# Mixer block with an MLP: the last output tile in three column pieces, and the instructions outside a block

## The chip, the cores and the metric

The kernel runs on one core of a Trainium2 chip. Its time is device time in microseconds (us), the median over several executions. The profile comes from one execution; its span runs from the first to the last recorded instruction of the program on that core. Engines are named as the profile names them: PE (matrix unit; PEld is its weight load), DVE (vector), ACT (activation), POOL (GpSimd) and SP (the engine that issues most DMAs).

## The reference

The input `x` has 2048 rows of 512 columns (bfloat16). Two stages follow one another:

```python
h  = gelu(layernorm(x) @ w1)                       # 512 -> 512
hs = concat(g0, g1, g2, g3) @ w2                   # four column quarters of h, shifted along the rows by +1, -1, +2, -2
x1 = x + hs
h2 = gelu(layernorm(x1) @ w3) @ w4                 # 512 -> 1792 -> 512
return x1 + h2
```

## The kernel before

The rows are cut into 16 tiles of 128. Stage 1 normalizes a tile (`ln`), transposes it, multiplies by `w1` (`mm_up`, layer 1) and evicts through the activation function into `hT`; `mm_mix` reads `hT` with shifted columns, multiplies by `w2`, and DVE adds `x`, which gives the tile `x1`. Stage 2 normalizes `x1`, multiplies by `w3` (`mm_up`, layer 2) into `h2T`, and `mm_down` multiplies by `w4`.

`mm_down(t)` is where an output tile is made. It is 14 matmuls on PE (one for each 128 rows of `w4`, line 511) that sum into one bank of `o_ps`, one DVE addition of `x1` that moves the sum to `o_sb` (line 519), and one store that SP issues (line 522). The last tile, 15, is made in column pieces whose widths stand in `TAIL`: each piece has its own bank, its own 14 matmuls `down15_0`, `down15_1`, its own addition `res15_0`, `res15_1` and its own store. The banks of `o_ps` are handed out in turn by `next_bank`, and there are two of them (`NOB = 2`).

The operations are not issued where they are written. `pg.add` records each with what it reads and writes, and `Program.order` puts them in an order for each engine: PE in the order of `SCRIPT`, which ends with `down:14-15`, the others by due times. `emit` then issues them in that order and places the waits. A wait is placed only where the engine does not already know that the event has come.

`emit` does this inside `nc.Block()`. The block gives each engine a body of its own; the engine's main body ends in a jump to it (lines 602 to 606), and the body ends in another jump (line 593) to a common end, where all five engines meet: each engine drains and reports to POOL on one semaphore, POOL waits for the four reports and then releases the four on another. A meeting of the same form also stands ahead of the kernel's first instruction (line 669); it belongs to the program's frame and not to `emit`. The last instructions of SP's body wait for the semaphore of every store (line 655).

Of the kernel before, what the change touches and what calls it, by code (L numbers as in the profile page):

```python
# [12 lines left out]
ENGINES = ["sp", "act", "pe", "dve", "pool"]  # L13
# [178 lines left out]
SQRT = (0,)  # L192
STAT_ACT = (1, 3, 6, 16, 23)
HALF = (0,)
TAIL = (256, 256)
LOADS = """
x2 x1 x0 x4-5 w1b w1a x3 w2 x6-7 w3 x8-11 x12-15 w4b tp19 w4a
"""
# [6 lines left out]
def bass_standalone__mixer_s_mlp__prompt_kernel(nc, x, w1, w2, w3, w4, out):  # L205
# [14 lines left out]
    with ExitStack() as es:  # L220
# [38 lines left out]
        def next_bank():  # L259
            nbank[0] += 1  # L260
            return (nbank[0] - 1) % NOB, nbank[0]
# [236 lines left out]
        def mm_down(t):  # L498
# [3 lines left out]
            c0 = 0  # L502
            for hh, W in enumerate(TAIL if last else (D,)):
                b, v = next_bank()
# [72 lines left out]
        pg.line(queue)  # L577
        pg.order()
        emit(nc, es, pg)

def emit(nc, es, prog):

    engs = {"sp": nc.sync, "act": nc.scalar, "pe": nc.tensor, "dve": nc.vector, "pool": nc.gpsimd}
    sems = {e: es.enter_context(nc.semaphore("sem_" + e)) for e in ENGINES}
    ndma = 0
    for op in prog.seq:
        if op.queue is not None:
            op.stream = ("dma", ndma)
            sems[op.stream] = es.enter_context(nc.semaphore(f"sem_dma{ndma}"))
            ndma += 1  # L590
        else:
            op.stream = op.eng
    with nc.Block() as block:
        bodies = {}

        def keep(name):
            def _body(e):
                bodies[name] = nc.cur_body

            return _body  # L600

        block.gpsimd(keep("pool"))
        block.sync(keep("sp"))
        block.scalar(keep("act"))
        block.vector(keep("dve"))
        block.tensor(keep("pe"))
        know = {e: {} for e in ENGINES}
        implied = {}
        count = {}
        last_write, readers = {}, {}  # L610
        for op in prog.seq:
            e = op.eng
            needs = {}

            def need(sv):
                if needs.get(sv[0], 0) < sv[1]:
                    needs[sv[0]] = sv[1]

            for res, ver in op.reads:
                lw = last_write[res]  # L620
                assert lw[2] == ver, (op.name, res, ver, lw)
                need(lw)
            for res, ver in op.writes:
                if res in last_write:
                    need(last_write[res])
                for sv in readers.get(res, ()):
                    need(sv)
            if e == "pe":
                needs.pop("pe", None)
            k = know[e]  # L630
            with nc.body(bodies[e]):
                for s, v in sorted(needs.items(), key=lambda sv: -sv[1]):
                    if k.get(s, 0) >= v:
                        continue
                    engs[e].wait_ge(sems[s], v)
                    for s2, v2 in implied[(s, v)].items():
                        if v2 > k.get(s2, 0):
                            k[s2] = v2
                    k[s] = max(k.get(s, 0), v)
                ins = op.fn(engs[e])  # L640
                inc = 1 if op.queue is None else 16
                ins.then_inc(sems[op.stream], inc)
            val = count[op.stream] = count.get(op.stream, 0) + inc
            snap = dict(k)
            snap[op.stream] = max(snap.get(op.stream, 0), val)
            implied[(op.stream, val)] = snap
            for res, ver in op.reads:
                readers.setdefault(res, []).append((op.stream, val))
            for res, ver in op.writes:
                last_write[res] = (op.stream, val, ver)  # L650
                readers[res] = []
        with nc.body(bodies["sp"]):
            for op in prog.seq:
                if op.name.startswith("out_dma"):
                    nc.sync.wait_ge(sems[op.stream], 16)


# [26 lines left out]
```

## Time and profile before

| what | us |
|---|---|
| median of 9 runs | 138.47 |
| lowest and highest of them | 137.95 and 139.11 |
| span of the profiled execution | 137.3 |
| the profiled execution's own time | 139.1 |

| engine | busy us | share of the span |
|---|---|---|
| PE | 131.4 | 96% |
| DVE | 58.8 | 43% |
| ACT | 51.4 | 37% |
| POOL | 19.5 | 14% |

The granted clock of PE is 0.999 of full speed. The time of an execution is 1.8 us longer than its span: what is done before the program's first recorded instruction and after its last lies outside the span. Waits and the issue of DMAs are not counted as busy; they are read from the views of single lines and of the waits. Records of sequencers carry a q (SPq, POOLq, PEldq).

### The profile page before, as it was taken

How to read it: one execution, taken by the hardware profiler on the slowest of the kernel's cores; microseconds unless marked ns; L12 is line 12 of the kernel's file. 1: busy time of each engine (PE TensorE's matmuls, PEld its weight loads, DVE VectorE, ACT ScalarE, POOL GpSimd, SP SyncE). 2: the span in 40 equal slices, each digit the busy share in tenths (PEclk: the TensorE clock that was granted, in tenths of full speed). 3: DMA queues.
4: the chain of work that ended last, by engine and by line, in shares of the span. 5: the costliest groups of instructions: out<-in, count | busy, mean ns of one | idle time of the engine just before them, and what ended most of it. 6: DMA issues, size and time to landing. Idle time of an engine off the chain costs nothing.

```text
span 137.3 us, 1989 instructions
## 1 busy us (share of the span) xinstructions
PE 131.4 (96%) x786; PEld 72.9 (53%) x786; DVE 58.8 (43%) x169; ACT 51.4 (37%) x70; POOL 19.5 (14%) x43
## 2 busy tenths in 40 slices
PE   6689999989999999999999999999999999999992
PEld 2287788756668644444444444444444444444471
DVE  1888899996899650044520053220002222322231
ACT  4799657432757545540055520025550000000000
POOL 2341483331142510001010000000000000000000
PEclk9999999999999999999999999999999999999999
DMA  3999964583279542001210002110001111111111
GB/s 111 299 357 410 354 212 98 115 81 76 40 183 205 114 99 54 0 0 38 81 38 1 0 0 70 44 38 5 0 0 36 40 38 38 43 38 38 67 48 41
DMA packets 21257, 12.19 MB, mean 89 GB/s; under 512 B 13568, under 2 KB 20736, under 8 KB 21248
## 3 DMA queue, kind: packets, MB, share of 16 engines
q1 hardware_dynamic: 21104, 12.00, 33.8%
q8 instruction: 6, 0.10, 0.3%
q10 hardware_dynamic: 144, 0.07, 0.2%
q14 instruction: 3, 0.02, 0.1%
HBM read 6.82 MB, written 2.10 MB: 65 GB/s over the span
## 4 chain that ended last, share of the span: by engine, by line
PE 83%; DVE 6%; DMA 5%; POOL 2%; SPq 1%; issue 1%; ACT 0%
PE y_ps L442 39%; PE o_ps L511 35%; PE o_ps L482 8%; DMA xnT<-xn_buf 3%; DVE st L349 3%; DMA x_sb<-in_x_dram 2%; POOL rstd L366 2%; DVE xn_buf L372 1%; PE y_ps L415 1%; POOL xn_buf L383 1%; SPq L296 1%; DVE mv L351 0%; DVE vpe L355 0%; DVE st6b L343 0%; DVE xnT L421 0%
## 5 line engine op out<-in xcount | busy, mean ns | idle before, releaser
L442 PE MATMUL y_ps<-xnT,w_sb 128*128 128x256 bf16 (+2 forms) x440 | 64.3, 305 | 0.5 <-DMA xnT<-xn_buf 0.5
L442 PEld LDWEIGHTS y_ps<-xnT,w_sb 128*128 128x128 bf16 x440 | 40.2, 98 | 24.6 <-issue 1.2
L511 PE MATMUL o_ps<-w_sb,h2T 128*128 128x512 bf16 (+1 forms) x238 | 48.9, 366 | 0.0
L457 ACT ACTIVATE h2T<-y_ps 128x1024 bf16<-128x1024 f32 (+1 forms) x29 | 28.6, 994 | 36.6 <-PE y_ps L442 36.6
L511 PEld LDWEIGHTS o_ps<-w_sb,h2T 128*128 128x128 bf16 x238 | 23.3, 98 | 25.3
L519 DVE TENSOR_TENSOR o_sb<-o_ps,x_sb 128x512 bf16<-128x512 f32 (+1 forms) x17 | 11.2, 660 | 44.6 <-PE o_ps L511 44.3
L366 POOL TENSOR_TENSOR rstd<-vpe,neghalf 128x1 f32<-128x1 f32 x31 | 17.0, 559 | 62.3 <-DVE vpe L355 50.3
L493 DVE TENSOR_TENSOR x_sb<-o_ps,x_sb 128x512 bf16<-128x512 f32 x14 | 9.6, 689 | 22.9 <-PE o_ps L482 22.9
L349 DVE BATCH_NORM_STATS2 st<-x_sb 128x6 f32<-128x512 bf16 x26 | 17.5, 685 | 2.2 <-DMA x_sb<-in_x_dram 2.1
L482 PE MATMUL o_ps<-w_sb,hT 128*128 128x512 bf16 x64 | 15.9, 379 | 0.0
L372 DVE TENSOR_SCALAR xn_buf<-x_sb,mv,rstd 128x512 bf16<-128x512 bf16 x25 | 10.2, 412 | 3.9 <-POOL rstd L366 2.8
L457 ACT ACTIVATE hT<-y_ps 128x1024 bf16<-128x1024 f32 (+1 forms) x10 | 8.4, 851 | 8.3 <-PE y_ps L442 8.2
L482 PEld LDWEIGHTS o_ps<-w_sb,hT 128*128 128x128 bf16 x64 | 6.1, 98 | 5.3
L535 PE MATMUL o_ps<-zeros 128*128 128x512 bf16 x12 | 4.1, 514 | 1.2 <-DVE zeros L269 1.2
L380 ACT ACTIVATE xn_buf<-x_sb,nmr,rstd 128x512 bf16<-128x512 bf16 x5 | 4.0, 810 | 2.6 <-DVE nmr L376 2.6
L351 DVE BATCH_NORM_AGGREGATE mv<-st 128x2 f32<-128x6 f32 x26 | 4.1, 173 | 0.2
L355 DVE TENSOR_SCALAR vpe<-mv 128x1 f32<-128x1 f32 x26 | 3.6, 148 | 0.3
L415 PE MATMUL y_ps<-ident,xn_buf 128*128 128x128 bf16 x28 | 2.4, 220 | 1.3 <-DVE xn_buf L372 1.2
L324 ACT ACTIVATE junk<-x_sb 128x512 bf16<-128x512 bf16 x5 | 3.1, 629 | 0.7 <-DVE x_sb L489 0.7
L535 PEld LDWEIGHTS o_ps<-zeros 128*128 128x128 bf16 x12 | 1.4, 125 | 3.4 <-issue 1.9
L415 PEld LDWEIGHTS y_ps<-ident,xn_buf 128*128 128x128 bf16 x28 | 1.8, 98 | 2.4 <-DVE xn_buf L372 2.0
L420 ACT ACTIVATE xnT<-y_ps 128x512 bf16<-128x512 bf16 (+1 forms) x5 | 2.6, 549 | 0.1
(33 smaller groups left out, 18.9 us busy)
## 6 DMA issues: line engine op xcount, KB each, us to landing
out_dram<-o_sb SPq DMA_DIRECT2D x15, 128.0 KB, 1.7
w_sb<-in_w_dram SPq DMA_DIRECT2D x1, 1792.0 KB, 9.8
w_sb<-in_w_dram SPq DMA_DIRECT2D x2, 896.0 KB, 9.4
x_sb<-in_x_dram SPq DMA_DIRECT2D x2, 512.0 KB, 11.3
x_sb<-in_x_dram SPq DMA_DIRECT2D x2, 256.0 KB, 4.5
w_sb<-in_w_dram SPq DMA_DIRECT2D x2, 256.0 KB, 3.5
w_sb<-in_w_dram SPq DMA_DIRECT2D x1, 512.0 KB, 5.6
x_sb<-in_x_dram SPq DMA_DIRECT2D x3, 128.0 KB, 2.4
```

Of the source, the lines that this page charges most:

```text
L349: pg.add("dve", f"bnst{q}", lambda e: e.bn_stats(st6[:, q, :], src), reads=rs, writes=[(("st6", q), 0)], dur=605)
L351: pg.add("dve", f"bnag{q}", lambda e: e.bn_aggr(mv[:, q, :], st6[:, q, :]), reads=[(("st6", q), 0)], writes=[(("mv", q), 0)], dur=75)
L366: lambda e: e.tensor_tensor(col(rstd), col(vpe), neghalf[:], ALU.pow),
L372: lambda e: e.tensor_scalar(dst, src, mv[:, q, 0:1], rstd[:, q : q + 1], ALU.subtract, ALU.mult),
L415: ins = e.transpose(chunk(c), xn_buf[:, slot(q), P * c : P * (c + 1)], ident[:])
L442: ins = e.matmul(y_ps[:, p, W * i : W * (i + 1)], wsb[:, dc, P * fc : P * (fc + 1)], src[:, dc, P * t0 : P * t0 + W], start=(dc == 0), sto ...
L457: (lambda d, s: (lambda e: e.activation(d, s, ACT_F.Gelu_apprx_tanh)))(dst, ysrc),
L482: ins = e.matmul(dst, hT[:, j, c0 : c0 + P], w2_sb[:, j, :], start=(j == 0), stop=(j == DC - 1))
L493: f = lambda e: e.tensor_tensor(x1_sb[:, t, :], dst, x_sb[:, t, :], ALU.add)
L511: ins = e.matmul(dst, h2T[:, fc, P * t : P * (t + 1)], w4_sb[:, fc, cs], start=(fc == 0), stop=(fc == FC - 1))
L519: (lambda d, c: (lambda e: e.tensor_tensor(o_sb[:, oi, c], d, x1_sb[:, t, c], ALU.add)))(dst, cs),
L535: ins = e.matmul(o_ps[:, b, :], zeros[:, 0:P], zeros[:], start=True, stop=True)
```

## The change

`TAIL` becomes `(256, 128, 128)`: the first piece of the last tile stays as it is, and the second is made as two pieces of 128 columns, each with 14 matmuls, an addition and a store. The third piece gets the bank that the first one had.

`emit` no longer opens a block. The same loop issues into the main body of each engine, so the five jumps at lines 602 to 606, the five at line 593 and the meeting of the engines at the end are gone. SP's waits for the stores are its last instructions; there are 18 stores instead of 17. The program's order on each engine is otherwise the same.

```diff
-TAIL = (256, 256)
+TAIL = (256, 128, 128)
...
-    with nc.Block() as block:
-        bodies = {}
-
-        def keep(name):
-            def _body(e):
-                bodies[name] = nc.cur_body
-
-            return _body
-
-        block.gpsimd(keep("pool"))
-        block.sync(keep("sp"))
-        block.scalar(keep("act"))
-        block.vector(keep("dve"))
-        block.tensor(keep("pe"))
-        know = {e: {} for e in ENGINES}
...
-            with nc.body(bodies[e]):
-                for s, v in sorted(needs.items(), key=lambda sv: -sv[1]):
...
-                    engs[e].wait_ge(sems[s], v)
...
-                ins = op.fn(engs[e])
...
-        with nc.body(bodies["sp"]):
-            for op in prog.seq:
-                if op.name.startswith("out_dma"):
-                    nc.sync.wait_ge(sems[op.stream], 16)
+    know = {e: {} for e in ENGINES}
...
+        for s, v in sorted(needs.items(), key=lambda sv: -sv[1]):
...
+            engs[e].wait_ge(sems[s], v)
...
+        ins = op.fn(engs[e])
...
+    for op in prog.seq:
+        if op.name.startswith("out_dma"):
+            nc.sync.wait_ge(sems[op.stream], 16)
```

More of the change, by code (lines that the diff above doesn't have):

```diff
@@ L592, in emit @@
             op.stream = op.eng
-    with nc.Block() as block:
-        bodies = {}
-        def keep(name):
-            def _body(e):
-                bodies[name] = nc.cur_body
-            return _body
-        block.gpsimd(keep("pool"))
-        block.sync(keep("sp"))
-        block.scalar(keep("act"))
-        block.vector(keep("dve"))
-        block.tensor(keep("pe"))
-        know = {e: {} for e in ENGINES}
-        implied = {}
-        count = {}
-        last_write, readers = {}, {}
-        for op in prog.seq:
[L612 to L630, printed above, removed]
-            with nc.body(bodies[e]):
-                for s, v in sorted(needs.items(), key=lambda sv: -sv[1]):
-                    if k.get(s, 0) >= v:
-                        continue
-                    engs[e].wait_ge(sems[s], v)
[L636 to L639, printed above, removed]
-                ins = op.fn(engs[e])
[L641 to L651, printed above, removed]
-        with nc.body(bodies["sp"]):
-            for op in prog.seq:
-                if op.name.startswith("out_dma"):
-                    nc.sync.wait_ge(sems[op.stream], 16)
@@ new lines, in emit, with need @@
+    know = {e: {} for e in ENGINES}
+    implied = {}
+    count = {}
+    last_write, readers = {}, {}
+    for op in prog.seq:
+        e = op.eng
+        needs = {}
+        def need(sv):
+            if needs.get(sv[0], 0) < sv[1]:
+                needs[sv[0]] = sv[1]
+        for res, ver in op.reads:
+            lw = last_write[res]
+            assert lw[2] == ver, (op.name, res, ver, lw)
+            need(lw)
+        for res, ver in op.writes:
+            if res in last_write:
+                need(last_write[res])
+            for sv in readers.get(res, ()):
+                need(sv)
+        if e == "pe":
+            needs.pop("pe", None)
+        k = know[e]
+        for s, v in sorted(needs.items(), key=lambda sv: -sv[1]):
+            if k.get(s, 0) >= v:
+                continue
+            engs[e].wait_ge(sems[s], v)
+            for s2, v2 in implied[(s, v)].items():
+                if v2 > k.get(s2, 0):
+                    k[s2] = v2
+            k[s] = max(k.get(s, 0), v)
+        ins = op.fn(engs[e])
+        inc = 1 if op.queue is None else 16
+        ins.then_inc(sems[op.stream], inc)
+        val = count[op.stream] = count.get(op.stream, 0) + inc
+        snap = dict(k)
+        snap[op.stream] = max(snap.get(op.stream, 0), val)
+        implied[(op.stream, val)] = snap
+        for res, ver in op.reads:
+            readers.setdefault(res, []).append((op.stream, val))
+        for res, ver in op.writes:
+            last_write[res] = (op.stream, val, ver)
+            readers[res] = []
@@ L659 @@
+    for op in prog.seq:
+        if op.name.startswith("out_dma"):
+            nc.sync.wait_ge(sems[op.stream], 16)
 _INS = ['x', 'w1', 'w2', 'w3', 'w4']
```

## The prediction

> **What bounds the kernel now.** I read the page's first part, then the chain of waits, the timeline of the last microseconds, and last the single lines of the end (655 and 593), which hold no busy time and so show in no sum.
>
> From the page, the span and the engines' busy time:
>
> ```profile
> span 137.3 us, 1989 instructions
> PE 131.4 (96%) x786; PEld 72.9 (53%) x786; DVE 58.8 (43%) x169; ACT 51.4 (37%) x70; POOL 19.5 (14%) x43
> ```
>
> PE fills the span except at its two ends, and the change touches only the ends. The chain in order of time (start, length, what):
>
> ```profile
> 0.72 0.39 SPq L296
> ...
> 1.64 2.96 DMA x_sb<-in_x_dram
> 4.62 0.43 DVE st6b L343
> ...
> 101.34 33.29 PE o_ps L511 x168
> 134.65 0.42 DVE o_sb L519
> ```
>
> It begins with SP's issue of the first loads, so what delays that issue delays everything. It ends with 33.29 us of unbroken PE and the last addition. What follows is not in the chain: 137.3 - (134.65 + 0.42) = 2.2 us of store and parting. The timeline of the last tile (start, length, engine, line, operation, then the idle time before it):
>
> ```profile
> 131.65 0.69 DVE L519 TENSOR_TENSOR o_sb<-o_ps,x_sb 128x512 bf16<-128x512 f32 x1 [2.39 <-PE o_ps L511]
> 133.12 0.42 DVE L519 TENSOR_TENSOR o_sb<-o_ps,x_sb 128x256 bf16<-128x256 f32 x1 [0.78 <-PE o_ps L511]
> 134.65 0.42 DVE L519 TENSOR_TENSOR o_sb<-o_ps,x_sb 128x256 bf16<-128x256 f32 x1 [1.10 <-PE o_ps L511]
> ```
>
> The two pieces are 1.53 us apart, PE's time for 14 matmuls of 256 columns. SP issues the last store at 135.10. Lines 655 (SP's waits for the stores) and 593 (the block's end), by instruction, with first and last start:
>
> ```profile
> L655 SPq EVENT_SEMAPHORE  x8: 28/28/28, 135.5 to 136.9; - x8
> L593 POOLq EVENT_SEMAPHORE  x2: 17/17/17, 137.1 to 137.2; - x2
> L593 SPq COMPARE_BRANCH  x1: 33/33/33, 136.9 to 136.9; - x1
> L593 SPq DRAIN  x1: 7/7/7, 137.1 to 137.1; - x1
> L593 PEldq EVENT_SEMAPHORE  x1: 51/51/51, 137.2 to 137.2; - x1
> ```
>
> SP's wait for the last store ends at 136.88 in the trace (last semaphore event at 136.84). Then come the jump at 136.92, SP's drain at 137.08, POOL's gathering at 137.11 and its release at 137.19, the last release at 137.24 plus 0.05. All of it, 137.30 - 136.88 = 0.41 us, stands after the last useful event.
>
> [...] The trace has 692 ns for 512 columns and 424 for 256[...]. [...] The jumps leave no record of their own here, but SP's release from the first meeting starts at 0.64 and lasts 0.02, and its first load is issued at 0.72: 0.07 us, room for one. [...]
>
> **The change, part by part** (against the profiled execution: span 137.30, time 139.1).
>
> *Five jumps at the start.* SP issues its first load one jump earlier[...] between 0 and the 0.07 that the trace has between release and issue. The chain above starts with this issue, so the shift is passed on whole; DVE, PE, ACT and POOL move with it.
>
> *PE in the tail.* Fourteen matmuls of 256 columns become 28 of 128. The pace at 128 columns is in the trace, from an early stage:
>
> ```profile
> 7.90 1.28 PE L442 MATMUL y_ps<-xnT,w_sb 128*128 128x128 bf16 x20
> ```
>
> A single one takes 0.22, so the pace is (1.28 - 0.22)/19 = 0.056 us, and 28 x 0.056 = 1.56 against 14 x 0.109 = 1.53 before: +0.04. Weight loads double to 28 at 98 ns each, and overlap as in that row.
>
> *The new bank wait.* `down15_2` takes the bank of `down15_0` and so waits for `res15_0`, which ends at 133.12 + 0.42 = 133.55. PE comes there at 132.92 (start of the second piece) + 14 x 0.056 = 133.70. From a DVE end to a waiting PE the trace has 0.05 (the memset of `zeros` ends at 1.11, PE starts at 1.16), so 0.10 us of cover is left and the wait costs nothing. Without it, `down15_2` with its 14 matmuls, then `res15_2` and the last store, would be late by as much. `res15_1` (from about 133.9 for 0.29) is done before `res15_2` is due at about 134.69.
>
> *DVE in the tail.* The last addition is 128 wide[...].
>
> *The last store.* SP issues three stores instead of two, 0.33 us each and over 0.7 us apart, so none queues behind another. The issues' sizes and median times to landing:
>
> ```profile
> out_dram<-o_sb SPq DMA_DIRECT2D x15, 128.0 KB, 1.7
> out_dram<-o_sb SPq DMA_DIRECT2D x2, 64.0 KB, 1.6
> ```
>
> By single issue the trace has 1.69 for most of 128 KB, 1.53 for the first of 64 KB, and 1.73 for the last, whose last semaphore event comes 0.17 after the one before it while a refill of instructions (8 KB, from 136.27 to 136.68) is under way. From 1.69 to 1.53 the 64 KB are worth 0.16, so 32 KB save 0.08. Packets of 256 B to HBM are not in the trace: bounds -0.25 (the late event goes too) and +0.25 (each packet costs twice its 27 ns at 512 B, 8 to an engine: 8 x 27 = 0.22). I take -0.08.
>
> *The end.* SP's nine waits of two semaphores each (one more than before) run about 0.06 us apart during the 1.6 us in which the last store is on its way; only the last counts, and with it the program ends. Jump, drains, gathering and release go: -0.41. The bounds are 0[...] and -0.9: the 0.41 and half a microsecond of what PE, DVE, ACT and POOL do after the program, which they now reach before SP does. I take -0.41 with the 1.8 us outside the span unchanged.
>
> Sum: -0.05 + 0.04 - 0.13 - 0.08 - 0.41 = **-0.63 us**, a span of 136.67. The profiled execution's 139.1 stands 0.6 above the median of the runs; the difference is carried over to the median: 138.47 - 0.63 = **137.84 us**, -0.45%.
>
> **The rivals.**
> 1. *The end costs the same elsewhere.* [...] only start and tail remain: -0.22, **138.25**. [...]
> 2. *More goes than the span shows.* Four engines have nothing to do well before the end (their drains at line 593 are done by 135.13); if what they do after the program shortens the 1.8 us, the gain is up to -0.63 - 0.5 = -1.1, **137.35**. Nothing in the profile divides the 1.8, so this is a bound.
> 3. *Slower[...].* Pieces 2 and 3 are 256 B on each partition. [...] the last store pays another round trip like its own of 1.4 us (first landing of the last store, 135.10 to 136.48): -0.63 + 1.4 = +0.8, **139.25**. It decides from 0.63 + 0.42 = 1.05 us of additional landing on. Against it: the step from 1024 to 512 B took the mean packet from 47 to 27 ns, with no sign of a fixed cost[...].
> 4. *The change doesn't do what it says*, because PE stalls in the bank wait or paces wider than 0.056: the tail's gain of 0.17 is used up, and -0.46 remains, **138.0**.
>
> **How the numbers follow.** About 0.3% (0.42 us) is what a measurement of this kernel can tell from no change. The forecast gets 0.56, rival 4 0.10, rival 1 0.18, rival 2 0.10, rival 3 0.06. The forecast with the store's and the start's bounds reaches from 137.6 to 138.1; a small part of it and a third of rival 4 fall within 0.3%. Faster: 0.54 + 0.07 + 0.10 = 0.71; same: 0.02 + 0.03 + 0.18 = 0.23; slower: 0.06. The range, 137.2 to 138.4, takes in rivals 1, 2 and 4 and leaves out rival 3.
>
> **What would show it.** In the profile after: no row of line 593's kind; SP's last wait as the end of the span, at about 136.7; 28 matmuls of 128 columns 0.056 apart without a gap before the third piece; additions of 0.42, 0.29 and 0.29; the last store landing in about 1.6; the first load issued at about 0.67. A span shortened by 0.6 and a time that isn't speaks for rival 1; a time shortened by more than the span for rival 2; a landing of the last store over 2 us for rival 3. I am wrong if the span loses less than 0.4 us.

## The result, and the profile after

The changed kernel takes 137.38 us (median of 16 runs, 137.01 to 138.47); the kernel before takes 138.51 in the runs beside it. The ratio is 0.9918, with a 95% interval of 0.9899 to 0.9938: 1.1 us faster, between 0.9 and 1.4. Forecast were 137.84 and a gain of 0.63. The time lies in the range, the sign is right, and the gain was taken for little more than half of what it is. (Ratios here and below leave out the few executions that were over 1.5% above the fastest of their kernel; medians of times count every execution.)

The page after, to set beside the one before:

```profile
span 137.1 us, 2008 instructions
PE 132.7 (97%) x800; PEld 73.5 (54%) x800; DVE 59.1 (43%) x170; ACT 51.5 (38%) x70; POOL 19.5 (14%) x43
```

Read against the 137.3 of before, this page shows a gain of 0.2. That comparison misleads. The chain of waits after (start, length, what) shows why:

```profile
0.72 0.40 SPq L296
...
1.65 3.32 DMA x_sb<-in_x_dram
5.00 0.43 DVE st6b L343
...
101.96 33.32 PE o_ps L511 x182
135.31 0.29 DVE o_sb L519
```

The first load is issued at 0.72, as before. But the wait for `x` took 3.32 us in this execution where it took 2.96 in the other, and the last stretch of PE begins at 101.96 instead of 101.34. Of these 0.62 us, 0.36 come from the first load; the rest comes in small pieces later, among them 0.12 in a transposing DMA (`xnT<-xn_buf`). That is the spread between executions, in a part that the change doesn't touch: the second traces of the two kernels enter the last tile at 130.65 and 131.33, the other kernels' between 130.1 and 132.5. It has to be cut off: I count from PE's first matmul of the last tile, 131.39 before and 132.01 after. From there the last tile's timeline after is (start, length, engine, line, operation, then the idle time before it):

```profile
133.74 0.42 DVE L519 TENSOR_TENSOR o_sb<-o_ps,x_sb 128x256 bf16<-128x256 f32 x1 [0.78 <-PE o_ps L511]
134.52 0.29 DVE L519 TENSOR_TENSOR o_sb<-o_ps,x_sb 128x128 bf16<-128x128 f32 x1 [0.36 <-PE o_ps L511]
135.31 0.29 DVE L519 TENSOR_TENSOR o_sb<-o_ps,x_sb 128x128 bf16<-128x128 f32 x1 [0.49 <-PE o_ps L511]
```

The additions have the three lengths foreseen, 0.78 us apart: 14 matmuls of 128 columns at 0.056, and no gap ahead of the third piece. SP's waits for the stores (first and last start):

```profile
L639 SPq EVENT_SEMAPHORE  x9: 28/28/28, 136.0 to 137.1; - x9
```

The last of these is the end of the program; no line of the block's end follows.

Two measures carry what comes now. The **tail** is the time from PE's first matmul of the last tile to the program's last recorded instruction, from single records of each trace. The **part outside the span** is an execution's time less its span; within one kernel it varies by no more than 0.08 around its median (spans of single executions are on record to 0.1, which makes up most of that), where the times of most of the kernels spread by more than 1 us.

| us | before | before, second trace | after | after, second trace |
|---|---|---|---|---|
| tile's start to the last addition's start | 3.26 | 3.26 | 3.29 | 3.29 |
| last addition | 0.42 | 0.42 | 0.29 | 0.29 |
| hand-over to SP | 0.03 | 0.03 | 0.03 | 0.03 |
| last store, issue to last landing | 1.73 | 1.53 | 1.47 | 1.47 |
| landing to the end of SP's wait | 0.05 | 0.04 | 0.04 | 0.04 |
| end of SP's wait to the end of the program | 0.41 | 0.42 | 0 | 0 |
| tail | 5.90 | 5.71 | 5.13 | 5.13 |
| outside the span, median of several runs | 1.82 | 1.83 | 1.35 | 1.38 |

Against the second trace of before the tail is 0.58 shorter, and the part outside is 0.47 shorter: 1.05 us together, which is the measured gain within its interval. Nearly half lies where no line of a profile stands. (The second traces are those of the last experiments below. The 1.82 of before is from the runs beside the first experiments, as the spans of the runs beside the first measurement are not on record.) The runs beside the second traces give the same split without any trace: their median span is 136.65 before and 136.1 after, 0.55 shorter, and the part outside is 0.45 shorter.

### The profile page after: what moved, and what is told of

It reads as the page before. It is cut to its first block, busy times and chain, and to the rows that moved or that the text cites. A ratio compares the mean times of both kernels' runs of the same rounds, so it can differ in the third digit from the quotient of the medians.

```text
span 137.1 us, 2008 instructions
## 1 busy us (share of the span) xinstructions
PE 132.7 (97%) x800; PEld 73.5 (54%) x800; DVE 59.1 (43%) x170; ACT 51.5 (38%) x70; POOL 19.5 (14%) x43
## 4 chain that ended last, share of the span: by engine, by line
PE 83%; DVE 6%; DMA 5%; POOL 2%; SPq 1%; issue 1%; ACT 0%
PE y_ps L442 39%; PE o_ps L511 35%; PE o_ps L482 8%; DMA xnT<-xn_buf 3%; DVE st L349 3%; DMA x_sb<-in_x_dram 2%; POOL rstd L366 2%; DVE xn_buf L372 1%; PE y_ps L415 1%; POOL xn_buf L383 1%; SPq L296 1%; DVE mv L351 0%; DVE vpe L355 0%; DVE st6b L343 0%; DVE xnT L421 0%
## 5 line engine op out<-in xcount | busy, mean ns | idle before, releaser
L511 PE MATMUL o_ps<-w_sb,h2T 128*128 128x512 bf16 (+2 forms) x252 | 48.9, 355 | 0.0
L519 DVE TENSOR_TENSOR o_sb<-o_ps,x_sb 128x512 bf16<-128x512 f32 (+2 forms) x18 | 11.4, 632 | 44.3 <-PE o_ps L511 44.1
L535 PE MATMUL o_ps<-zeros 128*128 128x512 bf16 x12 | 5.2, 626 | 1.2 <-DVE zeros L269 1.2
```

Source lines behind the costliest of these rows:

```text
L511: ins = e.matmul(dst, h2T[:, fc, P * t : P * (t + 1)], w4_sb[:, fc, cs], start=(fc == 0), stop=(fc == FC - 1))
L519: (lambda d, c: (lambda e: e.tensor_tensor(o_sb[:, oi, c], d, x1_sb[:, t, c], ALU.add)))(dst, cs),
L535: ins = e.matmul(o_ps[:, b, :], zeros[:, 0:P], zeros[:], start=True, stop=True)
```

## The experiments

My theory was that the parts add up, and that the part outside shrinks because PE, DVE, ACT and POOL, which have nothing to do during the last store, can now do there what they do after the program, while at the end of the block they had to wait for SP first. The rivals: the tail carries most of the gain; the jumps do; the part outside depends on something else.

### Only the widths

```diff
 # kernel before
-TAIL = (256, 256)
+TAIL = (256, 128, 128)
```

> Only the widths are changed (256, 128, 128); the block with its jumps and its meeting stays. My theory (the two parts add up, the tail being worth 0.1 to 0.3 us and the end of the block the rest): 138.3, ratio about 0.998, time outside the span 1.8 us as before, lines of the block's end unchanged. Rival theory (the tail carries most of the 1.1 us, for instance because the last store lands sooner by more than the profile of one execution shows): 137.7 or less, ratio 0.994 or less. In the profile: last addition 0.29, last store landed 1.47 to 1.65 after its issue, third piece without a gap on PE.

Measured: 138.69 us, ratio 0.9998 (0.9975 to 1.0022), outside 1.82. The runs don't resolve a gain; the interval holds both no gain and the 0.998 expected, and excludes the 0.994 of the rival. The trace resolves it: the tail is 5.55, with the last addition at 0.29, the last store landed after 1.48, and the end of the block unchanged. Three of the lines of that end (first and last start):

```profile
L593 POOLq EVENT_SEMAPHORE  x2: 17/17/17, 136.7 to 136.8; - x2
L593 SPq COMPARE_BRANCH  x1: 33/33/33, 136.5 to 136.5; - x1
L593 PEldq EVENT_SEMAPHORE  x1: 51/51/51, 136.8 to 136.8; - x1
```

5.55 is 0.16 under the second trace of before and 0.36 under the first. The widths are worth about 0.16 us by these traces, 0.1% of the time, too little for these runs to show alone.

### Only the block removed

```diff
 # changed kernel
-TAIL = (256, 128, 128)
+TAIL = (256, 256)
```

> Only the block is removed; widths stay 256 and 256. My theory: 137.65, ratio 0.994, of which 0.41 us lies in the span (SP's last wait is its end) and about 0.45 outside it (outside falls from 1.8 to about 1.35, because what the other four engines do after the program runs beside the last store). Rival (the end costs the same elsewhere, the change in the part outside the span is chance): 138.1, ratio 0.997, outside 1.8. The first load's issue stays at 0.72 if jumps cost nothing.

Measured: 137.79 us, ratio 0.9948 (0.9927 to 0.9969), outside 1.31. The tail is 5.29, 0.42 under the second trace of before; the first load is issued at 0.72. Both halves of the theory come out: 0.42 in the span and 0.51 outside, together 0.93. The runs' own gain is 0.7 with an interval from 0.4 to 1.0, which holds it near its upper end. The rival that the end costs the same elsewhere is out.

### A meeting put back, without jumps

```diff
 # changed kernel, end of emit
             nc.sync.wait_ge(sems[op.stream], 16)
+    nc.all_engine_barrier()
```

> The changed kernel (no block, no jumps) with a meeting of all five engines put back behind SP's last wait. It tells the jumps from the meeting. My theory (the meeting is all of it): the span is longer than the changed kernel's by 0.2 to 0.35 us, the part outside is back at about 1.8, in all 138.1 to 138.3, ratio to the kernel before about 0.998. Rival (the jumps to and from the body are what cost): the time stays within 0.2 us of the changed kernel, 137.4 to 137.6, ratio 0.993.

Measured: 138.11 us, ratio 0.9981 (0.9960 to 1.0001), outside 1.84. Three of the ten lines of this meeting:

```profile
L640 POOLq EVENT_SEMAPHORE  x2: 17/17/17, 135.8 to 135.9; - x2
L640 SPq DRAIN  x1: 7/7/7, 135.8 to 135.8; - x1
L640 PEldq EVENT_SEMAPHORE  x1: 51/51/51, 136.0 to 136.0; - x1
```

SP's last wait ends at 135.75 and the program at 136.00: the meeting by itself takes 0.25 us. In the kernel before the same stretch took 0.41 to 0.42; the remaining 0.16 is SP's jump, which stood between the wait and the drain (136.92 to 137.08 in the first trace; the jump's record also carries the wait for the first store, issued at 64.5 and landed long before). The tail is 5.39, 0.26 over the changed kernel's, and the part outside is back in full. The meeting, not the jumps, makes most of it.

### All engines end with SP, without a meeting

```diff
 # changed kernel, behind SP's waits
+    last = [op for op in prog.seq if op.name.startswith("out_dma")][-1]
+    for e in ("act", "dve", "pe", "pool"):
+        engs[e].wait_ge(sems[last.stream], 16)
```

> The changed kernel, in which ACT, DVE, PE and POOL too wait for the last store before they end, with no drains, gathering or release. All five engines thus leave the program at the same time as SP does. My theory (the engines' work after the program is hidden only where they leave early): the span stays at the changed kernel's (137.1 in a profile, within 0.1 of SP's last wait), but the part outside goes from 1.35 back to about 1.8, in all 137.8, ratio 0.995. Rival (the part outside depends on the meeting's own instructions or on SP alone): 137.4, ratio 0.992, outside 1.35.

Measured: 137.78 us, ratio 0.9941 (0.9917 to 0.9965), outside 1.86. The waits added, two of four:

```profile
L642 POOLq EVENT_SEMAPHORE  x1: 17/17/17, 136.7 to 136.7; - x1
L642 PEldq EVENT_SEMAPHORE  x1: 51/51/51, 136.7 to 136.7; - x1
```

They end within 0.04 us of SP's last wait, so the tail is 5.16, against 5.13. The part outside is nevertheless 0.5 longer than the changed kernel's. Nothing of the meeting is there, no drain, gathering or release: that the engines leave the program late is enough. This separates the theory from the rival, which had 1.35 here.

### Which engine is the slow one: the last store waited for by another engine

```diff
 # changed kernel, end of emit; E is "act", "dve", "pe" or "pool"
-    for op in prog.seq:
-        if op.name.startswith("out_dma"):
-            nc.sync.wait_ge(sems[op.stream], 16)
+    outs = [op for op in prog.seq if op.name.startswith("out_dma")]
+    for op in outs[:-1]:
+        nc.sync.wait_ge(sems[op.stream], 16)
+    engs[E].wait_ge(sems[outs[-1].stream], 16)
```

> The changed kernel, but the last store alone is waited for by ACT instead of SP; SP, DVE, PE and POOL end earlier. What ACT has to do[...] then stands in the part outside the span. Theory A (one of the four engines has a long way there, the others not): the part outside is either about 1.85 (ACT is the one) or 1.35 and less. Theory B[...]: values that differ from engine to engine in steps of about 0.1 between 1.35 and 1.85. Span as in the changed kernel.

> As the kernel with ACT, with DVE as the engine that waits for the last store. Theory A: outside about 1.85 if DVE is the long one, 1.35 or less if not. Theory B: a value between, different from that of ACT, PE and POOL by steps of about 0.1. Either way the time is 137.4 to 137.9 and never below the changed kernel's by more than the part outside falls.

> As the kernel with ACT, with PE as the engine that waits for the last store. Theory A: outside about 1.85 if PE is the long one, 1.35 or less if not. Theory B: a value between, different from the others by steps of about 0.1.

> As the kernel with ACT, with POOL as the engine that waits for the last store. Theory A: outside about 1.85 if POOL is the long one, 1.35 or less if not. Theory B: a value between, different from the others by steps of about 0.1. If one of these four has less outside than the changed kernel's 1.35, it is also faster than it by that difference.

| waits for the last store | time | ratio to before | outside the span | tail |
|---|---|---|---|---|
| SP (changed kernel) | 137.38 | 0.9918 (0.9899 to 0.9938) | 1.35 | 5.13 |
| DVE | 137.52 | 0.9924 (0.9895 to 0.9953) | 1.48 | 5.13 |
| ACT | 137.45 | 0.9920 (0.9899 to 0.9942) | 1.53 | 5.13 |
| PE | 137.57 | 0.9929 (0.9905 to 0.9952) | 1.59 | 5.17 |
| POOL | 137.95 | 0.9947 (0.9921 to 0.9973) | 1.88 | 5.13 |

The tails are equal to 0.04 and the parts outside are not: in steps, as Theory B said, for SP, DVE, ACT and PE, with one engine far behind as Theory A said, POOL. DVE, ACT and PE have four runs each (1.43 to 1.51, 1.51 to 1.58 and 1.56 to 1.65), and the changed kernel's own median moved by 0.03 between its two measurements: POOL's distance is sure, the steps between neighbours are small. POOL's 1.88 is near the 1.86 with all four late and the 1.82 of the kernel before, where POOL's last instruction ends 0.09 before the program does. So at the end of the block it was POOL that set the end of an execution: it needs about 0.53 us more than SP from its last instruction to the end (1.88 against 1.35), and the meeting held it back until SP was done. What makes the steps among the other engines is not shown by these runs. By the part outside, the changed kernel already has the best of the five; the times alone don't tell SP, DVE, ACT and PE apart.

### Other widths, and both kernels again, unchanged

```diff
 # changed kernel
-TAIL = (256, 128, 128)
+TAIL = (512,)          # one kernel
+TAIL = (448, 64)       # another
```

> The changed kernel with the last tile in one piece of 512 columns. Theory (the tail is worth the widths of its last addition and last store, and PE pays nothing for cutting): from PE's first matmul of the last tile to the end of the program 5.73 us against the changed kernel's 5.13: PE about the same to the end of its last matmul, addition 0.69 instead of 0.29, store 1.69 instead of 1.47. Time 138.0, 0.6 over the changed kernel. Rival (the end of the program is set by something that the widths don't touch): within 0.2 us of the changed kernel.

Measured in one piece: 138.04 us, ratio 0.9971 (0.9951 to 0.9990), 0.56 over the changed kernel beside it. The tail is 5.91 and not 5.73: the addition is as expected, but the last semaphore event of the last store came 0.23 behind the one before it, 1.93 after the issue. Without that late event the tail would be 5.68, 0.55 over the changed kernel's, which is what the medians show; so the event may have been this execution's.

```profile
133.99 0.69 DVE L519 TENSOR_TENSOR o_sb<-o_ps,x_sb 128x512 bf16<-128x512 f32 x1 [2.27 <-PE o_ps L511]
134.71 0.33 SPq L522 DMA_DIRECT2D out_dram<-o_sb  x1
```

> The changed kernel with pieces of 448 and 64 columns. It asks if narrower is better still. If the pace of PE goes with the columns (about 0.03 us at 64), [...] the store about 1.43, and the tail is 5.0, 0.1 below the changed kernel's 5.13. If the pace stays near the 0.056 of 128 columns because the weight load sets it, PE takes 14 x 0.026 = 0.36 more and the tail is 5.4, the time 137.6 to 137.7. I expect the second.

Measured: 138.58 us, ratio 1.0006 (0.9984 to 1.0028): all of the gain gone, in a way that I had not expected. The timeline, and the view of line 522 on landing:

```profile
134.21 1.52 PE L511 MATMUL o_ps<-w_sb,h2T 128*128 128x448 bf16 x19
135.36 0.76 DVE L519 TENSOR_TENSOR o_sb<-o_ps,x_sb 128x448 bf16<-128x448 f32 x2 [1.90 <-PE o_ps L511]
136.01 0.81 SPq L522 DMA_DIRECT2D out_dram<-o_sb  x2
```

```profile
DMA to landing us min/median/max: 1.7/1.7/2.3
```

PE was not slowed: matmuls of 64 columns start 0.029 apart (135.158, 135.186, 135.215), so the weight load doesn't set a floor at 0.056, and my second case is wrong. But 14 of them last only 0.41 us, less than the 0.63 of the addition of 448 columns, which is still running when the last piece is summed. The second addition follows at once and ends at 136.12, and SP, which issued the first store at 136.01, can issue the second only at 136.39, 0.27 after its data is ready. The issue takes 0.43 instead of 0.33, and the last event comes 2.27 after its start, 0.74 behind the one before. This execution entered the last tile late (132.51), so I use only its tail: 6.19, 1.06 over the changed kernel's. Of this, about 0.25 is the wait for the issue and 0.80 the store, for the most part its late last event. The packet records show a part of that lateness: eight of the store's 128 data packets start only at 137.77 to 137.84, the others by 137.53, while a refill of instructions (8 KB) is moved from 137.28 to 137.78. That is 0.3 of the 0.74; where the rest comes from is not shown. The medians of the two kernels' times differ by about as much as the tails, 138.58 against 137.48, so the loss is not this one execution's; that the late event recurs in every execution is likely, but only this one was traced.

> The changed kernel as it is, beside the two with other widths, as their measure. 137.4, ratio to the kernel before 0.992, part outside the span 1.35, tail 5.13.

Measured: 137.48 us, ratio 0.9919 (0.9893 to 0.9944), outside 1.38, tail 5.13. As expected.

> The kernel before as it is, for a second trace of it: was the last store's landing of 1.73 us, with its last semaphore event 0.17 behind the one before, its habit or one execution's? Habit: again about 1.73, and the tail from PE's first matmul of the last tile is 5.90. Chance: 1.54 as in the kernel with only the block removed, tail 5.70.

Measured: 138.17 in this one run, and a tail of 5.71: the last store landed after 1.53. So the 1.73 is not the kernel's habit: its two traces differ, and the 1.54 of the kernel with only the block removed agrees with the second.

## Why the prediction was right or wrong

**Start, -0.05: wrong, it is 0.** SP's release starts at 0.64 and its first load at 0.72 with the jump and without it, in every trace. The 0.07 from the end of the one to the other, in which I saw "room for one", is there without a jump too. The bounds, 0 to 0.07, held 0; that a jump takes 0.05 here was not shown by any trace.

**PE, +0.04, and the bank wait, 0: right.** The last addition starts 0.04 later after the tile's start than before (3.29 against 3.26), and the third piece follows without a gap (its matmuls start 0.055 to 0.056 apart from the first on).

**Last addition, -0.13: right,** 424 to 292 ns. The trace before has 692 ns for 512 columns and 424 for 256, and a straight line through these two gives 290 for 128.

**Last store, -0.08: about right.** 1.53 to 1.47 is -0.06; the 1.73 that I measured from was an execution's accident, named in the bounds. Rival 3, which adds 1.4 us to the landing of the last store, is out: the store landed 1.47 after its issue, and its packets of 256 B took 17.6 ns on average in the trace after, where those of 512 B took 27. One reading was off: the three stores are not all "over 0.7 us apart" but 0.65 and 0.78, as the prediction's own figures for the additions' ends give; at 0.33 us an issue none queues all the same.

**The end, -0.41: right inside the span, wrong in the whole.** The span's part is 0.41. The term that failed is the sentence "with the 1.8 us outside the span unchanged": it went to 1.35. The bound of -0.9 that I gave for this step is what happened (-0.41 - 0.47 = -0.88), and so rival 2 was the case, at 137.35 almost to the number, with a chance of 0.10 where the forecast had 0.56. That the measured time lies in the range is owed to the range, which was drawn to take in this rival, and not to the forecast's sum. I knew that four engines were idle before the end, and took the absence of a view for the absence of an effect. The experiments put POOL's name to it; what POOL does in that time no view shows.

**Sum.** 0 + 0.04 - 0.13 - 0.06 - 0.42 - 0.47 = -1.04 by the traces and the parts outside, against -1.13 and -1.04 by the medians of the two measurements. The two edits are unequal: about 0.16 for the widths and 0.9 for the block by the traces and parts outside (by the runs alone 0.0 and 0.7, each to within about 0.3).

**Rivals 1 and 4** are out: the part outside fell rather than rose, and PE neither stalled nor slowed. My criterion "I am wrong if the span loses less than 0.4 us" was badly put: the first pair of pages shows 0.2, because one execution entered the last tile 0.62 later than the other. The median spans, 0.55 apart, pass it; a tail counted from a fixed event would have been the right measure for single traces.

## What to carry to other kernels

An engine that is done early should be let go: a meeting of all engines behind the last store cost 0.25 us of its own here (0.41 with SP's jump) and also made the part outside the span half a microsecond longer (1.84 us with a meeting, 1.35 without); one engine was enough to wait for the last store, here best SP and worst POOL. A last output piece was worth narrowing here as long as the next addition, the issue queue and PE kept pace: 512, 256 + 256 and 256 + 128 + 128 gave tails of 5.91 (5.68 without its late event), 5.29 and 5.13, but 448 + 64 gave 6.19: the big piece's addition and store then stand in front of the small one's (0.25 of the loss), and the last store's last event came late (the most of it, with a cause that is open in part). To judge a change of some tenths at the end, count from an event near it and look at time less span as well as at the span.

## What the runs showed of the hardware

- The way from an engine's last instruction to the end of an execution differs by engine: with SP last 1.31 to 1.38 us lie outside the span, with DVE 1.48, ACT 1.53, PE 1.59, POOL 1.88.
- Jumps at the start cost nothing that can be seen (from the start of SP's release to the start of its first issue 0.085 us with and without); the jump between SP's last wait and its drain, which also carried a wait long fulfilled, cost 0.16.
- A refill of instructions (8 KB) falls beside the last store in all five traces of one or two pieces, and beside the store of tile 14 in all nine of three pieces. The store beside it had its last semaphore event late by between 0 and 0.74 us (before: 0.17 and 0.01; block removed: 0.00; one piece: 0.23; 448 and 64: 0.74). With three pieces tile 14's store landed after 1.96 to 2.19 instead of 1.70, and nobody waited for that. Moving the refill may thus be part of what the third piece brings; no run tried it alone.
- Matmuls of 64 columns run at 0.029 us, those of 128 at 0.056 and of 448 at 0.189: the pace goes with the columns down to 64.
